# Block-sparse attention and a Fourier mixing layer on one core: whitened tiles fetched back one by one, turned tiles laid out tile by tile

## The chip, the core and the metric

The kernel runs on one core of one Trainium2 chip. A core has five engines with queues of their own: TensorE (PE in the profile, its weight loads PEld), VectorE (DVE), ScalarE (ACT), GpSimd (POOL), and SyncE (SP), which here issues nearly all DMA transfers. An engine takes its instructions in order; an instruction that waits for a semaphore holds up all that stand behind it on the same engine. The metric is the device time of one launch in microseconds.

## The reference

Four batches; in each, eight heads of attention over 768 positions, 64 wide, under a mask of 32 x 32 blocks. The output goes, as x of 768 x 512, through a Fourier mixing layer with a two-layer network behind it.

```python
scores = scale * np.matmul(q, k.transpose(0, 1, 3, 2))
scores = np.where(mask, scores, -1000000000.0)
attn = softmax(scores); attn_out = np.matmul(attn, v)
x = attn_out.transpose(0, 2, 1, 3).reshape(B, S, H * D)      # 4 x 768 x 512
u = x + np.real(np.fft.fft(np.fft.fft(x, axis=1), axis=2))
un = (u - mean(u)) / np.sqrt(var(u) + 1e-06)                 # along the 512
return u + np.maximum(un @ w_ch1, 0.0) @ w_ch2               # 512 x 2048, 2048 x 512
```

## The kernel before

**Tiles.** The 768 rows of a batch are two halves of three tiles of 128 rows (`half` 0 and 1, m = 0, 1, 2, T = 3). The mixing layer works in place on `xA` and `xB`, one for each half. `across` and `arrive` add the transform, `spread` takes mean and variance of a tile (POOL makes the reciprocal root), `whiten` makes the whitened tile `un` (128 x 512).

**Turning.** The product with `w_ch1` needs the whitened rows turned, as `unT[half]`: 128 partitions (a slice of the 512 features), 4 slices k, 384 rows. In the last batch PE turns each tile (`un_flip`). In batches 0, 1 and 2 PE is spared: `un_blocks` (L1009 to L1016) transposes 32 x 32 blocks on DVE and writes the tile to memory (`far`, one SP transfer of 256 KB); when all six tiles are written, `un_back` (L1018 to L1029) reads both halves back with 2 x 4 SP transfers of 192 KB in runs of 32 numbers (128 bytes), which puts the blocks in their places.

**Products.** `quad` computes four 128 x 384 blocks of the hidden layer by seven products in place of eight (Winograd's scheme). It needs sums of the four quarters of the turned matrix: `right(j)`, j = 1 to 4, four DVE subtractions (L1057), each half of the features and 384 rows wide, 128 x 768 elements in batches 0 to 2. The first two products of a quad (`xp`, `yp`) read `unT` as it is; the third (`z`) needs `right` 1 and 2, later ones 3 and 4. `channels` is the second layer, six tiles y in a round of two quads (L1268), four rounds in a batch. A round may instead be done by seven products on 256 columns (`round_of`, L1211, with sums on POOL, DVE and ACT): `seven[r]` is set if `state["alone"]` holds when the round's first quad is issued, and never for the last round.

**Order.** The order on every engine is written out by the program itself. Attention of batch b + 1 is interleaved with the mixing of batch b. A planner keeps a clock for each engine (`when`) with prices in the code. `late` holds the quads and channel steps that still are to be issued (PE's big work), `apart` the steps that prepare the next batch, each with a number `need`: it may go only when `len(late)` is not larger. The steps of list `before` in `mixer` (transform, whitening, `un_blocks`) carry a number that always allows them; those of `after` (`un_back`, the sums of weights `left`, `right`) carry `hold` = 6: they wait until only the last six channel steps of the batch in work are left, since `unT` has two buffers and the quads of the batch in work read both. `gap` takes steps from `apart` as long as the planner's DVE clock is not too far ahead of PE's. A step of kind "b" (`right`) is also held until PE's or DVE's clock is near `state["back"]`, which `un_back` sets to now + `BACK[b]` (13, 12, 15 us).

**Attention around it.** For each pair of heads and 128 keys a unit: `scores` (L579, two units are a group of 8 matmuls in the trace), ACT `Exp`, then, once channel steps are being issued, a DVE product with the mask (L609, tile `e`), in the first phase a mask product on PE (L589) instead; POOL adds up `e` (L639) and `values` (L653, tile `o`) multiplies with v. Scores have two PSUM slots, so a unit waits until `e` of the unit two before is made. A finished `o` is transposed by DVE into `oT` (L661, one buffer), and SP carries it to its place through memory (`row<-oT` L692, `x<-row` L696). SP also loads q, k and v (L231, L271) and stores the output (L1279).

**Also touched.** `scale_x` (L766) divides x by the sums of the softmax (kind "d", six steps a batch), `invert` (tile `st`, L751) turns the sums on PE before it, `spare_room` gives `right` and `left` their space. `general`, a second path for large scores, is not taken with these inputs.

Of the kernel before, what the change touches and what calls it, by code (L numbers as in the profile page):

```python
# [11 lines left out]
FP32 = mybir.dt.float32  # L12
# [87 lines left out]
def kernel(  # L100
# [14 lines left out]
    nc = tc.nc  # L115

    B, H, S, D = q.shape
    DM = H * D
    FF = w_ch1.shape[1]
    P = 128  # L120
    C = S // P
    BLK = 32
    NB = S // BLK
    NR = sampled_blocks.shape[1]
    HS = S // 2
    KS = cos_s.shape[1]
    KD = cos_d.shape[1]
    ND = DM // P
    NF = FF // P
    T = C // 2  # L130
# [51 lines left out]
    tr_p = ctx.enter_context(tc.tile_pool(name="tr_p", bufs=2))  # L182
# [3 lines left out]
    far_p = ctx.enter_context(tc.tile_pool(name="far_p", bufs=1, space=bass.MemoryType.DRAM))  # L186
# [7 lines left out]
    when = {"PE": 0.0, "ACT": 0.0, "DVE": 0.0, "POOL": 0.0}  # L194
# [18 lines left out]
    def room(i, shape, name, dtype=FP32):  # L213
        return big.tile(shape, dtype, tag=f"big{i}", name=name)
# [86 lines left out]
    def bit(n):  # L301
# [5 lines left out]
                      in_=bass.AP(tensor=_words(sampled_blocks, NB * NR), offset=0,  # L307
                                  ap=[[0, NB], [1, 2 * NB * NR]]))
# [135 lines left out]
    for w, w_sb in ((w_ch1, w1_sb), (w_ch2, w2_sb)):  # L444
        rows, cols = w.shape
        words = _words(w, rows * cols)
        for row in range(rows // P):
            for col in range(0, cols, WN):
                src = bass.AP(tensor=words, offset=2 * (row * P * cols + col),
                              ap=[[2 * cols, P], [1, 2 * WN]])  # L450
# [532 lines left out]
    def mixer(b, xA, xB):  # L983


        uns, unT = {}, {}
# [2 lines left out]

        def un_flip(half, m):  # L990
            if half not in unT:
                unT[half] = tr_p.tile([P, ND, T * P], FP32, tag="tr", name="unT")
            un = uns.pop((half, m))
            tag, pool = (("t", ps_t), ("m", ps_m))[half == 1 and m != 0]
            tp = pool.tile([P, ND, P], FP32, tag=tag, name="utp")
            for d in range(ND):
                nc.tensor.transpose(tp[:, d, :], un[:, d * P:(d + 1) * P], ident)
            nc.scalar.copy(out=unT[half][:, :, m * P:(m + 1) * P], in_=tp)

# [3 lines left out]

        lines = {}

        def un_blocks(half, m):  # L1010

            un = uns.pop((half, m))
            if half not in lines:
                lines[half] = far_p.tile([T, P, DM], FP32, tag=f"un{half}", name="far")
            nc.vector.transpose(out=un, in_=un)
            nc.sync.dma_start(out=lines[half][m], in_=un)  # L1016

        def un_back():  # L1018

            for half in range(2):  # L1020
                unT[half] = tr_p.tile([P, ND, T * P], FP32, tag="tr", name="unT")
                of = lines[half].rearrange("m (g j) (k a i) -> a j k (m g) i",
                                           j=BLK, a=P // BLK, i=BLK)
                for a in range(P // BLK):
                    nc.sync.dma_start(
                        out=unT[half][BLK * a:BLK * a + BLK].rearrange(
                            "j k (g i) -> j k g i", i=BLK),
                        in_=of[a])
            state["back"] = max(when["PE"], state["ready"]) + BACK[b]  # L1029

        t, s = {}, {}
        K1, K2 = slice(0, ND // 2), slice(ND // 2, ND)

        def spare_room():
            if s:
                return
            rest, n, w = room(5, [P, ND * HS], "t4"), HS * ND // 2, P * ND // 2
            t[4] = rest[:, 0:n].rearrange("p (k n) -> p k n", n=HS)
            for i in (1, 3, 4):
                s[i] = rest[:, n:n + w].rearrange("p (k n) -> p k n", n=P)  # L1040
                n += w

        def right(j, *tiles):

            spare_room()
            if 1 not in t:
                both = room(4, [P, ND, HS], "t12")
                t[1], t[2], t[3] = both[:, K1, :], both[:, K2, :], unT[1][:, K1, :]
            b11, b21 = unT[0][:, K1, :], unT[0][:, K2, :]
            b12, b22 = unT[1][:, K1, :], unT[1][:, K2, :]  # L1050

            def part(ap):
                return ap.rearrange("p k (t n) -> p k t n", n=P)[:, :, tiles[0]:tiles[-1] + 1, :]

            to, a, c = {1: (t[1], b12, b11), 2: (t[2], b22, t[1]), 3: (b12, b22, b12),
                        4: (t[4], b21, t[2])}[j]
            tt(out=part(to), in0=part(a), in1=part(c), op=ALU.subtract)  # L1057
# [24 lines left out]
        def quad(p):  # L1082

            g = p // 2 % 2 if last else 0
            if p % 2 == 0:
                for i in range(2):
                    hs[g, i] = room((2, 0)[g] + i, [P, 4, HS], "h" + "AB"[i])
            if not last:
                if p % 2 == 0:
                    seven[p // 2] = state["alone"] and p // 2 < NF // 4 - 1  # L1090
                elif seven[p // 2]:
                    state["drain"]()
                    sums_room()
                    for j in (1, 2, 4, 3):
                        round_right(p // 2, j)
            l1, l2 = 2 * (p % 2), 2 * (p % 2) + 1
            h11, h12, h21, h22 = (hs[g, i][:, l, :] for l in (l1, l2) for i in range(2))
            a11, a12, s2, a22 = blocks(p)
            b11, b21, b22 = unT[0][:, K1, :], unT[0][:, K2, :], unT[1][:, K2, :]

            def product(to, a, c, after=0.0):
                for k in range(ND // 2):
                    nc.tensor.matmul(to, a[:, k, :], c[:, k, :], start=(k == 0),  # L1103
                                     stop=(k == ND // 2 - 1))
                return busy("PE", PRODUCT, after) + HOP

            def plus(to, ps, a, at):
                tt(out=to, in0=ps, in1=a, op=ALU.add)  # L1108
                return busy("DVE", SUM, at) + HOP

            def relu(h, at):
                nc.scalar.activation(out=h, in_=h, func=ACT.Relu)  # L1112
                busy("ACT", RELU, at)

            def combine(j):
                left(p + 1, j)
                busy("DVE", COMBINE)

            x, at = ps_m.tile([P, 512], FP32, tag="m", name="xp")[:, 0:HS], bank("m")
            z5, z7 = (ps_s.tile([P, 2, 512], FP32, tag="s", name=name)[:, 0, 0:HS]  # L1120
                      for name in ("z5", "z7"))
            done = product(x, a11, b11)
            nc.scalar.copy(out=h11, in_=x)
            p1 = busy("ACT", RELU, done) + HOP
            give(at, p1 - HOP)
            y, at = ps_m.tile([P, 512], FP32, tag="m", name="yp")[:, 0:HS], bank("m")
            p2 = product(y, a12, b21)
            done = product(z7, s2, t[2])
            u2 = plus(h21, z7, h11, max(done, p1))
            c11 = plus(h11, y, h11, p2)  # L1130
            relu(h11, c11)
            done = product(z5, s[1], t[1])
            plus(h12, z5, h21, done)
            combine(1)
            done = product(z7, s[3], t[3], u2)
            u3 = plus(h21, z7, h21, done)
            c22 = plus(h22, z5, h21, done)
            z_at[0] = c22
            relu(h22, c22)
            combine(3)  # L1140
            gap(0.0, 1.9)
            done = product(y, a22, t[4], c11)
            c21 = plus(h21, y, h21, done)
            give(at, c21 - HOP)
            relu(h21, c21)
            gap(0.0, 1.9, "t")
            done = product(z7, s[4], b22, u3)
            z_at[1] = plus(h12, z7, h12, done)
            relu(h12, z_at[1])
            combine(4)  # L1150
            if last:
                for j in ((1, 2), (3, 4))[p % 2]:
                    output_right(p // 4, j, p // 2 % 2)
            elif p % 2 == 1 and seven[p // 2]:
                state["soon"] = 0.4
# [243 lines left out]
        le = [("d", lambda i=i: left(0, i), 0.0, 0.0, COMBINE) for i in (1, 3, 4)]  # L1399
# [3 lines left out]
        if not last:  # L1403
            before = first + [pq[1], ar[0][1], ar[1][1], sp[0][1],
                              pq[2], wh[0][1], ft[0][1], ar[0][2], ar[1][2], sp[0][2],
                              pq[0], wh[0][2], ft[0][2], ar[0][0], ar[1][0], sp[0][0],
                              sp[1][1], wh[0][0], ft[0][0], sp[1][2], wh[1][1], ft[1][1],
                              sp[1][0], wh[1][2], ft[1][2], wh[1][0], ft[1][0]]
            after = ([("-", un_back, 0.0, 0.0, 0.0)] + le +
                     [("b", lambda i=i: right(i, 0, 1, 2), 0.0, 0.0, 1.0 if b else 1.7)  # L1410
                      for i in (1, 2, 3, 4)])
        rest = []
        for r in range(2 if last else 0):
            rest += [(lambda p=p: quad(p), 7 * PRODUCT) for p in range(4 * r, 4 * r + 4)]
# [12 lines left out]
    MOST, LEAST = 9.6, 2.5  # L1427
    COVER = 100.0
    AHEAD = 2.2
    BACK = 13.0, 12.0, 15.0  # L1430
    ALONE = 3.0
    LEAVES = 13.0
    SP = UP // SLOT
# [396 lines left out]
```

## Time and profile before

| what | value |
|---|---|
| median of 3 runs | 1061.15 us (1060.93 to 1061.73) |
| the profiled execution, its own time | 1062.32 us |
| its span, first to last instruction | 1060.2 us |
| mean granted TensorE clock | 0.986 |
| DVE busy | 712.8 us, 67% |
| ACT, POOL busy | 373.2 us, 327.3 us |
| `y` L1268, 336 matmuls of 512 columns | 75.2 + 75.1 us in two groups |
| `z<-unT,t` L1103, 256 matmuls of 384 columns | 93.3 us |
| `far<-un` / `unT<-far` | 18 transfers of 256 KB / 24 of 192 KB |

The span is divided as the program is: first attention of batch 0 alone (the first `scale_x` starts at 135.8 us), then phases in which the mixing of one batch overlaps with attention of the next, and at the end the mixing of the last batch alone (the last `scale_x` starts at 803.6 us). A line of the view in order of time gives start, duration, engine, source line, operation, output and inputs, count, and in brackets how long the engine was idle before it and what released it.

### The profile page before, as it was taken

What the parts mean: (1) busy time and instruction counts of PE and PEld (TensorE: products, weight loads), DVE (VectorE), ACT (ScalarE), POOL (GpSimd) and SP (SyncE); (2) the same over time, 40 slices, a digit from 0 to 9 for tenths busy, and PEclk for the clock granted to TensorE, in tenths of its full rate; (3) what the DMA queues carried; (4) which work ended last, traced back from release to release, by engine and by line L of the source; (5) the groups of instructions that cost most, each with busy time, mean ns of one, the idle gap of its engine ahead of it and who ended that gap; (6) DMA issues with size and microseconds to landing.
All of it is one profiled execution on the core that took longest, in us unless ns stands there. A gap on an engine that the chain in (4) does not pass through costs nothing.

```text
span 1060.2 us, 13059 instructions
## 1 busy us (share of the span) xinstructions
PE 1014.9 (96%) x4526; PEld 564.1 (53%) x4526; DVE 712.8 (67%) x1292; ACT 373.2 (35%) x763; POOL 327.3 (31%) x363
## 2 busy tenths in 40 slices
PE   8999999999999999799999999869999999999996
PEld 4333345435776853344544764334454764578575
DVE  6898795969776567574579477656357575674663
ACT  6978755563122223343241223333120221210210
POOL 1000183565733306373354222743340221000000
PEclk9999999999999999899999999989999999999998
DMA  7857522292000014732120002731000001000001
GB/s 213 233 168 220 113 46 45 50 141 35 1 1 1 1 46 115 104 64 46 30 45 1 1 11 72 137 65 23 11 18 10 1 1 41 19 1 1 0 17 47
DMA packets 163461, 58.12 MB, mean 55 GB/s; under 512 B 144172, under 2 KB 154170, under 8 KB 163386
## 3 DMA queue, kind: packets, MB, share of 16 engines
q1 hardware_dynamic: 162134, 56.45, 23.9%
q8 instruction: 38, 0.62, 0.3%
q10 hardware_dynamic: 1220, 0.72, 0.3%
q14 instruction: 37, 0.30, 0.1%
q0 software_dynamic: 32, 0.01, 0.0%
HBM read 43.80 MB, written 13.37 MB: 54 GB/s over the span
## 4 chain that ended last, share of the span: by engine, by line
PE 82%; DVE 7%; ACT 3%; POOL 2%; DMA 2%; issue 2%; SPq 2%; DVEq 0%; ACTq 0%; POOLq 0%
PE z L1103 16%; PE y L1268 12%; PE s L579 10%; PE o L653 8%; PE yp L1103 8%; PE yy L1336 7%; PE xp L1103 4%; PE yz L1211 3%; PE yw L1211 2%; PE yc L1211 2%; PE zp L861 2%; DVE e L609 1%; POOL acc L639 1%; PE s L589 1%; ACT e L599 1%
## 5 line engine op out<-in xcount | busy, mean ns | idle before, releaser
L639 POOL TENSOR_TENSOR acc<-acc,e 128x384 f32<-128x384 f32 x162 | 165.8, 1056 | 84.8 <-DVE e L609 62.2
L579 PE MATMUL s<-qT,kT 64*128 64x384 f32 x768 | 157.6, 525 | 28.8 <-DVE e L609 22.3
L653 PE MATMUL o<-e,vr 128*64 128x384 f32 x768 | 143.0, 499 | 0.0
L579 PEld LDWEIGHTS s<-qT,kT 64*128 64x128 f32 x768 | 64.7, 188 | 112.2 <-DVE e L609 42.7
L607 ACT ACTIVATE s<-s 128x768 f32<-128x768 f32 x86 | 65.7, 793 | 133.2 <-PE s L579 125.7
L639 POOL TENSOR_TENSOR acc<-e 128x384 f32<-128x384 f32 x40 | 44.7, 1137 | 212.7 <-ACT e L599 125.2
L609 DVE TENSOR_TENSOR e<-s,mask 128x768 f32<-128x768 f32 x86 | 78.3, 948 | 36.7 <-ACT s L607 31.1
L599 ACT ACTIVATE e<-s 128x768 f32<-128x768 f32 x106 | 80.9, 811 | 53.3 <-PE s L589 34.9
L1103 PE MATMUL z<-unT,t 128*128 128x384 f32 x256 | 93.3, 487 | 0.8 <-DVE hA L1108 0.8
L653 PEld LDWEIGHTS o<-e,vr 128*64 128x64 f32 x768 | 48.0, 137 | 71.0 <-issue 68.6
L1108 DVE TENSOR_TENSOR hA<-z,hA 128x384 f32<-128x384 f32 x64 | 35.6, 556 | 67.0 <-PE z L1103 66.9
L1112 ACT ACTIVATE hA<-hA 128x384 f32<-128x384 f32 x64 | 33.5, 523 | 123.4 <-DVE hA L1108 123.4
L1268 PE MATMUL y<-w_sb,hB 128*128 128x512 f32 x168 | 75.2, 596 | 0.0
L1268 PE MATMUL y<-w_sb,hA 128*128 128x512 f32 x168 | 75.1, 595 | 0.0
L1224 POOL TENSOR_TENSOR x<-of,x 128x256 f32<-128x256 f32 x45 | 34.8, 780 | 125.2 <-ACT of L1216 85.2
L1103 PEld LDWEIGHTS z<-unT,t 128*128 128x128 f32 x256 | 48.4, 190 | 35.6 <-DVE hA L1108 2.4
L1271 DVE TENSOR_TENSOR x<-y,x 128x512 f32<-128x512 f32 x42 | 28.9, 688 | 54.8 <-PE y L1268 54.8
L1112 ACT ACTIVATE hB<-hB 128x384 f32<-128x384 f32 x64 | 33.5, 523 | 86.3 <-DVE hB L1108 86.3
L1268 PEld LDWEIGHTS y<-w_sb,hB 128*128 128x128 f32 x168 | 31.1, 190 | 38.8 <-issue 38.6
L1268 PEld LDWEIGHTS y<-w_sb,hA 128*128 128x128 f32 x168 | 31.1, 190 | 37.3 <-issue 36.0
L1103 PE MATMUL xp<-unT,w_sb 128*128 128x384 f32 x128 | 49.9, 515 | 0.0
L1103 PE MATMUL yp<-unT,w_sb 128*128 128x384 f32 x128 | 47.4, 493 | 0.0
(236 smaller groups left out, 1703.8 us busy)
## 6 DMA issues: line engine op xcount, KB each, us to landing
wraw<-in_moe_w_ch_dram SPq DMA_DIRECT2D x32, 512.0 KB
vr<-in_v_dram SPq DMA_DIRECT2D x30, 192.0 KB
far<-un SPq DMA_DIRECT2D x18, 256.0 KB
unT<-far SPq DMA_DIRECT2D x24, 192.0 KB
qb<-in_q_dram SPq DMA_DIRECT2D x44, 96.0 KB
kb<-in_k_dram SPq DMA_DIRECT2D x44, 96.0 KB
out_dram<-x SPq DMA_DIRECT2D x11, 252.0 KB
out_dram<-x SPq DMA_DIRECT2D x18, 128.0 KB
```

Of the source, the lines that this page charges most:

```text
L579: nc.tensor.matmul(s[:, i, 0:HS], kT[rows, c * P:(c + 1) * P], qT[rows, queries], start=True, stop=u not in by_pe)
L599: nc.scalar.activation(out=e, in_=s[:, :, 0:HS], func=ACT.Exp, scale=scale)
L607: nc.scalar.activation(out=s[:, :, 0:HS], in_=s[:, :, 0:HS], func=ACT.Exp, scale=scale)
L609: nc.vector.tensor_tensor(out=e, in0=s[:, :, 0:HS], in1=m.broadcast_to([P, 2, HS]), op=ALU.mult)
L639: nc.gpsimd.tensor_add(out=acc[:, i, :], in0=start[:, i, :], in1=e[:, i, :])
L653: nc.tensor.matmul(o[D * i:D * i + D, :], vt[:, i, c, :], e[:, i, :], start=(c == 0), stop=(c == C - 1))
L1103: nc.tensor.matmul(to, a[:, k, :], c[:, k, :], start=(k == 0), stop=(k == ND // 2 - 1))
L1108: tt(out=to, in0=ps, in1=a, op=ALU.add)
L1112: nc.scalar.activation(out=h, in_=h, func=ACT.Relu)
L1211: nc.tensor.matmul(to, a[:, k, :], c[:, k, :], start=start and k == 0, stop=k == 1, skip_group_check=True)
L1268: nc.tensor.matmul(y, hs[0, half][:, l, m * P:(m + 1) * P], w2_sb[:, 4 * r + l, :], start=(l == 0), stop=(l == 3))
L1336: nc.tensor.matmul(ps, a[:, k, :], c[k // 2][:, k % 2, :] if isinstance(c, list) else c[:, k, :], start=(k == 0), stop=(k == 3))
```

## The change

`far` becomes one tile of memory for each (half, m). `un_blocks` appends each written tile to a queue `sent`; as soon as fewer than six steps are left in `late`, a call first fetches every tile that was queued before it, so a tile is fetched one tile after it was written. `fetch` reads one tile with four transfers of 64 KB, again in runs of 128 bytes. `un_back` fetches what is left and sets `state["back"]` to now + 9 us. `unT` is laid out tile by tile (128 x 3 x 4 x 128); the 384 columns of a product are three runs of 128. `right` is called for tiles 1 and 2 first, all four sums, then `un_last` adds 2 us to `state["back"]`, then for tile 0. `un_flip` of the last batch and `quad` follow the new layout.

```diff
-            nc.scalar.copy(out=unT[half][:, :, m * P:(m + 1) * P], in_=tp)
+            nc.scalar.copy(out=unT[half][:, m, :, :], in_=tp)
...
-        lines = {}
+        lines, sent = {}, deque()
+
+        def fetch(half, m):
+            if half not in unT:
+                unT[half] = tr_p.tile([P, T, ND, P], FP32, tag="tr", name="unT")
+            of = lines[half, m].rearrange("(g j) (k a i) -> a j k g i",
+                                          j=BLK, a=P // BLK, i=BLK)
+            for a in range(P // BLK):
+                nc.sync.dma_start(
+                    out=unT[half][BLK * a:BLK * a + BLK, m, :, :].rearrange(
+                        "j k (g i) -> j k g i", i=BLK),
+                    in_=of[a])
 
         def un_blocks(half, m):
             un = uns.pop((half, m))
-            if half not in lines:
-                lines[half] = far_p.tile([T, P, DM], FP32, tag=f"un{half}", name="far")
+            lines[half, m] = far_p.tile([P, DM], FP32, tag=f"un{half}{m}", name="far")
             nc.vector.transpose(out=un, in_=un)
-            nc.sync.dma_start(out=lines[half][m], in_=un)
+            nc.sync.dma_start(out=lines[half, m], in_=un)
+            while sent and len(late) < 2 * T:
+                fetch(*sent.popleft())
+            sent.append((half, m))
 
         def un_back():
-            for half in range(2):
-                unT[half] = tr_p.tile([P, ND, T * P], FP32, tag="tr", name="unT")
-                of = lines[half].rearrange("m (g j) (k a i) -> a j k (m g) i",
-                                           j=BLK, a=P // BLK, i=BLK)
-                for a in range(P // BLK):
-                    nc.sync.dma_start(
-                        out=unT[half][BLK * a:BLK * a + BLK].rearrange(
-                            "j k (g i) -> j k g i", i=BLK),
-                        in_=of[a])
-            state["back"] = max(when["PE"], state["ready"]) + BACK[b]
+            while sent:
+                fetch(*sent.popleft())
+            state["back"] = max(when["PE"], state["ready"]) + BACK[0]
+
+        def un_last():
+            state["back"] += BACK[1]
...
+        def by_k(half, ks):
+            return unT[half][:, :, ks, :].rearrange("p m k n -> p k m n")
...
             def part(ap):
-                return ap.rearrange("p k (t n) -> p k t n", n=P)[:, :, tiles[0]:tiles[-1] + 1, :]
+                return ap[:, :, tiles[0]:tiles[-1] + 1, :]
...
-            after = ([("-", un_back, 0.0, 0.0, 0.0)] + le +
-                     [("b", lambda i=i: right(i, 0, 1, 2), 0.0, 0.0, 1.0 if b else 1.7)
-                      for i in (1, 2, 3, 4)])
+            on = [[("b", lambda i=i, m=m: right(i, *m), 0.0, 0.0, us) for i in (1, 2, 3, 4)]
+                  for m, us in (((1, 2), 1.2), ((0,), 0.7))]
+            after = ([("-", un_back, 0.0, 0.0, 0.0)] + le + on[0] +
+                     [("-", un_last, 0.0, 0.0, 0.0)] + on[1])
...
-    BACK = 13.0, 12.0, 15.0
+    BACK = 9.0, 2.0
```

More of the change, by code (lines that the diff above doesn't have):

```diff
@@ L997, in un_flip @@
                 nc.tensor.transpose(tp[:, d, :], un[:, d * P:(d + 1) * P], ident)
-            nc.scalar.copy(out=unT[half][:, :, m * P:(m + 1) * P], in_=tp)
-        lines = {}
+            nc.scalar.copy(out=unT[half][:, m, :, :], in_=tp)
+        lines, sent = {}, deque()
+        def fetch(half, m):
+            if half not in unT:
+                unT[half] = tr_p.tile([P, T, ND, P], FP32, tag="tr", name="unT")
+            of = lines[half, m].rearrange("(g j) (k a i) -> a j k g i",
[5 more added lines that the diff above has]
+                    in_=of[a])
@@ L1018, in un_back @@
+            sent.append((half, m))
         def un_back():
-            for half in range(2):
-                unT[half] = tr_p.tile([P, ND, T * P], FP32, tag="tr", name="unT")
-                of = lines[half].rearrange("m (g j) (k a i) -> a j k (m g) i",
-                                           j=BLK, a=P // BLK, i=BLK)
-                for a in range(P // BLK):
-                    nc.sync.dma_start(
-                        out=unT[half][BLK * a:BLK * a + BLK].rearrange(
-                            "j k (g i) -> j k g i", i=BLK),
-                        in_=of[a])
@@ L1037, in spare_room @@
             rest, n, w = room(5, [P, ND * HS], "t4"), HS * ND // 2, P * ND // 2
-            t[4] = rest[:, 0:n].rearrange("p (k n) -> p k n", n=HS)
+            t[4] = rest[:, 0:n].rearrange("p (k m n) -> p k m n", m=T, n=P)
             for i in (1, 3, 4):
@@ L1045, in right @@
             spare_room()
+            b11, b21, b12, b22 = (by_k(h, ks) for h in range(2) for ks in (K1, K2))
             if 1 not in t:
[L1047 to L1050, printed above, removed]
+                both = room(4, [P, ND, T, P], "t12")
+                t[1], t[2], t[3] = both[:, K1], both[:, K2], b12
             def part(ap):
-                return ap.rearrange("p k (t n) -> p k t n", n=P)[:, :, tiles[0]:tiles[-1] + 1, :]
+                return ap[:, :, tiles[0]:tiles[-1] + 1, :]
             to, a, c = {1: (t[1], b12, b11), 2: (t[2], b22, t[1]), 3: (b12, b22, b12),
@@ L1098, in quad @@
             a11, a12, s2, a22 = blocks(p)
-            b11, b21, b22 = unT[0][:, K1, :], unT[0][:, K2, :], unT[1][:, K2, :]
+            b11, b21, b22 = by_k(0, K1), by_k(0, K2), by_k(1, K2)
             def product(to, a, c, after=0.0):
                 for k in range(ND // 2):
-                    nc.tensor.matmul(to, a[:, k, :], c[:, k, :], start=(k == 0),
+                    nc.tensor.matmul(to, a[:, k, :], c[:, k], start=(k == 0),
                                      stop=(k == ND // 2 - 1))
```

## The prediction

> **What bounds the kernel now.** I read the page's engine rows and its chain first, then PE in order of time, looking for bracketed waits, then DVE and SP at the same moments, and last the DMA load.
>
> ```profile
> PE 1014.9 (96%) x4526; PEld 564.1 (53%) x4526; DVE 712.8 (67%) x1292; ACT 373.2 (35%) x763; POOL 327.3 (31%) x363
> ...
> PE 82%; DVE 7%; ACT 3%; POOL 2%; DMA 2%; issue 2%; SPq 2%; DVEq 0%; ACTq 0%; POOLq 0%
> ```
>
> PE is the bound. The time is PE's work plus PE's waits, so an edit counts only if it alters one of the two. After 150 us PE has two long waits, both where one batch's quads follow another's. Batch 1, PE and then DVE:
>
> ```profile
> 429.48 1.78 PE L579 MATMUL s<-qT,kT 64*128 64x384 f32 x8 [1.29 <-DVE e L609]
> 431.18 2.80 PE L653 MATMUL o<-e,vr 128*64 128x384 f32 x16
> 440.15 2.93 PE L579 MATMUL s<-qT,kT 64*128 64x384 f32 x8 [6.17 <-DVE e L609]
> 443.01 2.93 PE L1103 MATMUL xp<-unT,w_sb 128*128 128x384 f32 x4
> ```
>
> ```profile
> 428.49 1.79 DVE L609 TENSOR_TENSOR e<-s,mask 128x768 f32<-128x768 f32 x2
> 435.54 0.96 DVE L1057 TENSOR_TENSOR t<-unT 128x768 f32<-128x768 f32 x1 [5.26 <-DMA unT<-far]
> ...
> 439.14 1.81 DVE L609 TENSOR_TENSOR e<-s,mask 128x768 f32<-128x768 f32 x2
> ```
>
> PE waits for `e`, `e` stands on DVE behind `right`, and `right` waits for the fetched tiles. After the wait PE runs at half speed: 8 score matmuls take 2.93 us, `xp` 2.72 (443.01 to 445.73) where 1.29 is usual. Batch 2, PE, DVE and SP:
>
> ```profile
> 682.74 1.78 PE L579 MATMUL s<-qT,kT 64*128 64x384 f32 x8 [1.29 <-DVE e L609]
> ...
> 697.93 2.93 PE L579 MATMUL s<-qT,kT 64*128 64x384 f32 x8 [8.40 <-DVE e L609]
> ```
>
> ```profile
> 692.86 0.58 DVE L661 STREAM_TRANSPOSE oT<-o 128x384 f32<-128x384 f32 x1 [5.57 <-DMA row<-oT]
> 693.36 0.91 DVE L1057 TENSOR_TENSOR t<-unT 128x768 f32<-128x768 f32 x1
> ```
>
> ```profile
> 673.69 11.10 SPq L1025 DMA_DIRECT2D unT<-far  x8
> 684.89 3.54 SPq L231 DMA_DIRECT2D qb<-in_q_dram  x4
> 688.53 2.74 SPq L692 DMA_DIRECT2D row<-oT  x4
> ```
>
> ```profile
> 676.00:680.00 4.00, 4.00 (x24) 1.54 (x22) 3.18 (x5) 1.74 (x3) 3.62 (x5) 1.00 1.00 132
> ```
>
> Here DVE waits because `oT` has one buffer, whose copy stood on SP behind eight fetches (11.1 us). The last columns of the window are clock, DMA share 1.00 and 132 GB/s: the burst of fetches is limited by the DMA engines, 1.5 MB in 11.1 us, not by SP.
>
> **The change, batch 1.** From the last quad's end (382.42) to the next quad 60.6 us pass. Their work: six y of 3.44 (20.6), three `pq` (2.1), nine score groups of 1.49 (13.4), o (9.8), `xt` and `sp` (1.6), 47.5 in all. So 13.1 are lost there, and 1.6 in the slow `xp` and `yp`: 14.7. Built, the changed kernel has on PE between these quads y y y, s, xt, s, o, s, y, sp, y, y: 27.7 us of work and one wait like that of 0.90 at 404.18. With Q for the last quad's end, the next quad is due at Q+28.6. Are the tiles there? Five tiles are written while `late` still holds six steps or more, so nothing is fetched early: SP issues all 24 fetches together behind the sixth write. DVE ends that tile at Q+4.9 (statistics .65, whiten .55, wait for POOL, whiten .55, y sum .69, transpose .71), three stores hold SP until Q+5.7, the write until Q+6.1. Twenty of 24 fetches at the burst's pace take 9.4 us and land 3.7 later (in the trace: last issue over at 431.8, DVE released at 435.54): tiles 1 and 2 at Q+19.2, tile 0 at about Q+21.1. On DVE `right` stands behind the sum of the fourth y, at Q+21.7, so it does not wait, and the first `z`, at Q+31.2, finds its sums made: the last needs 5.4 us of DVE from the tiles' arrival, so there are 6.6 us to spare. Six score groups move between later quads, where the trace has four groups and their o's in 11.81 us for 11.57 of work; I charge 0.4. Gain 14.7 - 0.9 - 0.4 = **13.4**.
>
> **Batch 2.** Lost now: 1.29 + 8.40, the slow groups 1.44 (2.93 for 1.49) and 0.67 (16 o matmuls 3.40 for 2.73): 11.8. Changed, four tiles are fetched between the writes. Moving down SP's rows with 2.2 to 2.4 us for four fetches (0.55 each, as `qb` loads of 96 KB cost at the least; a `row` transfer of 48 KB costs 0.62), each group delays the stores and `kb` loads behind it; the last write goes out at 675.2 in place of 673.3, and the last eight fetches are out at 680. Tiles 1 and 2 land near 680, tile 0 near 683. On DVE `right` for tiles 1 and 2 stands before `e` of the eighth group: after `kT` (681.76) 4 x 0.68 (the 512-wide rows of the last batch), then 0.95 of `e`: the next group starts at 685.4, PE having been free since 681.2. A wait of 4.2 replaces 1.29 and 8.40. `row<-oT` goes out by 686 and lands by 688, before `oT` is wanted (690). The other two groups follow the first quad. Gain 7.6; PE's clock may drop in 4.2 us of idling: in the windows it fell about 2.5 us into the wait of 8.40 and 5.4 into that of 6.17, each drop costing some 2.5; I take 1.5 of it. Gain **6.1**.
>
> The Trainium skill (TensorE: Matmul & The Clock Gate, "Why this matters for your kernels") warns of gaps over about 3 us. By it the drop comes for certain and the gain is 5.1; by the waits of 1.69 and 1.29, after which groups ran at speed, only short gaps are safe.
>
> **Batch 0.** Nothing waits here now, and this is where the change costs. Tiles come some 7 us sooner, so the planner puts the first quad before the last score groups, and DVE gets, one behind another from 234.0: four 512-wide sums, two 256-wide, the softmax sums (L708), two more, one `acc`, the reciprocal, and five `scale_x`, before the quad's first addition. Next to POOL `right` took 1.56 to 1.76 here against 0.95 later, a factor 1.7: 4 x 0.68 x 1.7 + 2 x 0.42 x 1.7 + 0.5 = 6.5, so `st` waits until 240.6 and not 239.6: **1.0**. Then 1.4 + 0.9 + 0.4 + 5 x 0.8 (0.68 to 0.93 alone) brings the addition to an end at 247.9; the product that needs it is due at 246.1: **1.8**. With 1.71 a `scale_x` (the pair of 3.42 at 254.5) it would be 6.3; POOL has no weight sums here now, so I take the low end.
>
> **Rounds.** This first quad no longer runs with `alone` set, so one round goes from 84 matmuls of 256 columns (0.2165 each, 18.2 us) to 48 of 512 (0.4295, 20.6): **+2.4**. One mask group of PE goes to DVE: **-0.4**. Folds of the next batch must now fit behind two quads and this round; they need about 20 us of DVE beside 20.6 of PE: **+0.3**.
>
> **At nothing.** Two-part sums cost DVE 4.4 for 3.8 us a batch, under PE's quads (without that cover 0.6 a batch). 48 more transfers and SP's waits for each write to land (before the next fetch) hold `qb`, `kb`, `vr`, `row` and stores behind them; in batch 0 `qb` slips from 219 to 222 and is wanted by ACT at 228.45. The last batch's turned tiles keep their sizes. A product over three runs of 128 columns has no row; three separate matmuls of 128 (0.110 each) would be 0.330 for 0.322, at most 8 ns on 512 matmuls, 4.1 us; none shorter is conceivable. The two-run DVE rows scale with size alone, so I take 0.
>
> **Sum:** -13.4 - 6.1 + 2.8 + 2.4 - 0.4 + 0.3 = -14.4. Span 1060.2 becomes 1045.8; the profiled execution, 1062.32 with 2.1 around the span, 1047.9. It lay 1.2 above the runs' median, so the median becomes **1046.8**.
>
> **Rivals.**
> *The wait in batch 2 stays as a wait for tiles* (SP's chain slips: four `kb` loads took 6.81 us at 658.15, where two 256 KB writes had just gone out, and more traffic may do the same to fetches; against: DMA share there is 0.36). Gain of batch 2 gone: 1053.
> *Batch 0 takes the dear `scale_x`* (6.3 for 1.8) and a clock drop (2.5): 1054. For: DVE rows doubled beside POOL; against: POOL's list has fewer sums there.
> *A fetch costs per transfer, not per byte* (slower). Place: SP's 24 issues in batch 1. At the 1.29 us that a fetch takes now, twenty take 25.8, tiles 1 and 2 land at Q+35.6, 9.8 later than the Q+25.8 that `z` allows, and the clock drops: batch 1 gains 0.9, not 13.4; batch 2's tiles come 12 later and its gain of 6.1 becomes a loss of 4: -14.4 + 12.5 + 10.1 = +8.2, 1069. It begins to hurt at 0.86 us a fetch and undoes the gain near 1.15. For: equal times of six of the eight fetches. Against: the first two, before the engines fill, take 0.65 and 0.77, and 48 KB takes 0.62.
> The Trainium skill (DMA: Bandwidth & Descriptors, "Anatomy of one DMA", for transfers that GpSimd issues) gives each a fixed 2 us; were none of it overlapped, 24 would take 48. The 0.62 of back-to-back rows says that it overlaps.
> *It does not do what it says*: in batch 1 nothing is fetched one by one, and if the order there brings the same wait, batch 2's gain pays for batch 0 and the round: about 1060.
>
> **Chances.** Forecast 0.58 (1041 to 1051), batch 2's wait 0.15, batch 0 0.09, price per transfer 0.14, no effect 0.04. The range 1041 to 1058 holds the first three. 0.2% (2 us) is what a measurement can tell from no change. Faster 0.82, same 0.04, slower 0.14.
>
> **What would show it.** Right: batch 1's quads about 29 us behind the last quad of batch 0, no DVE wait for `unT` over 1 us, fetch rows near 0.5 us, four rounds of `yc`, PE waits of 1 to 2 us before `st` and the third `z` of batch 0, one of about 4 us in batch 2. Wrong: fetch rows over 0.9 us, half clock before a batch's first quad, `L1103` rows above 486 ns with `unT` moving.

## The result: slower by 1.1 per cent, and the profile after

| what | before | after |
|---|---|---|
| median of 4 runs | 1061.26 us (1060.93 to 1061.73) | 1072.91 us (1072.56 to 1073.99) |
| ratio to before, 95% interval | | 1.0111 (1.0094 to 1.0129) |
| span of the profiled execution | 1060.2 us | 1072.0 us |
| mean granted clock | 0.986 | 0.979 |
| rounds of seven products, of all | 5 | 4 |

The prediction was 1046.8 us and faster. The time is 11.7 us longer, not 14.4 shorter.

The engine rows and the chain of the changed kernel's page:

```profile
PE 1020.5 (95%) x4486; PEld 557.9 (52%) x4486; DVE 712.6 (66%) x1294; ACT 369.4 (34%) x754; POOL 305.7 (29%) x344
...
PE 79%; DVE 11%; SPq 3%; ACT 3%; issue 2%; DMA 1%; POOL 1%; ACTq 0%; DVEq 0%
```

VectorE's busy time has not moved (712.8 before), but its share of the chain grew from 7 to 11 per cent: PE waits for it more, though it does not work more. The view of PE in order of time, changed kernel, between the quads of batch 0 and those of batch 1 (the last quad ends at 389.51):

```profile
423.72 2.93 PE L579 MATMUL s<-qT,kT 64*128 64x384 f32 x8 [17.79 <-DVE e L609]
426.58 5.20 PE L1280 MATMUL y<-w_sb,hB 128*128 128x512 f32 x8
...
439.46 1.45 PE L1115 MATMUL xp<-unT,w_sb 128*128 128x384 f32 x4
```

One wait of 17.79 us, and half clock behind it: eight score products take 2.86 us (1.49 is usual), eight of `y` 5.13 (3.44 is usual). Follow the bracket to VectorE, ScalarE and SP, the same view of each of these queues:

```profile
422.71 1.82 DVE L609 TENSOR_TENSOR e<-s,mask 128x768 f32<-128x768 f32 x2 [19.19 <-ACT s L607]
...
432.42 0.68 DVE L1069 TENSOR_TENSOR t<-unT 128x512 f32<-128x512 f32 x1
```

```profile
420.66 0.48 ACT L677 COPY x<-xt 128x384 f32<-128x384 f32 x1 [18.29 <-DMA out_dram<-x]
...
421.87 1.50 ACT L607 ACTIVATE s<-s 128x768 f32<-128x768 f32 x2
```

```profile
396.01 19.96 SPq L1016 DMA_DIRECT2D unT<-far  x24
416.08 2.50 SPq L1291 DMA_DIRECT2D out_dram<-x  x4
```

Read backwards: PE waits for `e`, `e` for the exponentials, and these stand on ScalarE behind the copy `x<-xt`. That copy begins the x of batch 2 in the buffer in which batch 0's x still lies (`xp` has two buffers), so it waits until batch 0's first half is stored. Four of these stores stand on SP behind 24 fetches, which hold it for 19.96 us. The fetched tiles themselves are in time: `t<-unT` at 432.42 waits for nothing.

While the block is issued, the windows (PE, its weight loads, VectorE, ScalarE and GpSimd in us, each with its count; then clock, DMA share, GB/s) show this:

```profile
404.00:408.00 4.00, 1.93 (x12) 0.48 (x8) 0.00 (x0) 0.00 (x0) 2.60 (x3) 1.00 0.62 97
...
412.00:416.00 4.00, 0.00 (x0) 0.00 (x0) 0.00 (x0) 0.00 (x0) 0.00 (x0) 0.50 0.62 97
```

The DMA engines are 62% busy, where the burst of batch 2 in the kernel before had 1.00. The block goes at SP's pace: 0.635 us (median of 72 rows) for a transfer of 64 KB. In this block twenty of the 24 took 0.58 to 0.64 us, and the second to the fifth 1.40 to 1.66, for a reason that no run here shows.

Batch 2, PE and then VectorE of the changed kernel:

```profile
703.72 2.93 PE L579 MATMUL s<-qT,kT 64*128 64x384 f32 x8 [5.29 <-DVE e L609]
```

```profile
698.73 1.46 DVE L1069 TENSOR_TENSOR t<-unT 128x512 f32<-128x512 f32 x1
700.23 1.36 DVE L1069 TENSOR_TENSOR t<-unT,t 128x512 f32<-128x512 f32 x1
701.51 0.68 DVE L1069 TENSOR_TENSOR unT<-unT 128x512 f32<-128x512 f32 x1
702.12 0.68 DVE L1069 TENSOR_TENSOR t<-unT,t 128x512 f32<-128x512 f32 x1
702.72 1.81 DVE L609 TENSOR_TENSOR e<-s,mask 128x768 f32<-128x768 f32 x2
```

This is the forecast wait: the four sums for tiles 1 and 2 stand ahead of `e`. Here no fetch is late either.

**Where the 11.8 us of span are.** For each row of PE take the distance to the start of the next row, less its count times the usual distance for its kind (lower quartile over the kernels of this study). What is left is waiting and slow clock. In us, by stretch; the two columns on the right are experiments below:

| stretch | before | after | after_back13 | back_13_12_9 |
|---|---|---|---|---|
| up to the second quad of batch 0 | 13.5 | 17.7 | 13.8 | 14.5 |
| rest of batch 0's quads | 3.5 | 2.5 | 3.2 | 3.0 |
| last quad of batch 0 to second of batch 1 | 16.1 | 23.0 | 12.2 | 13.1 |
| rest of batch 1's quads | 2.6 | 4.3 | 2.7 | 2.3 |
| last quad of batch 1 to second of batch 2 | 16.9 | 15.7 | 16.7 | 15.0 |
| from there to the end | 5.7 | 4.3 | 7.0 | 6.0 |

The sums are 58.3 before and 67.5 after, 9.2 more. With 2.4 for the round that is no longer done by seven products this makes 11.6 of 11.8. The sums of the two experiments, 55.6 and 53.9, lie 2.7 and 4.4 below the one before, while their spans are 4.3 and 4.0 shorter: a column is good to about 1.5 us.

### The profile page after: what moved, and what is told of

Same layout as the page of the kernel before. It is cut to its first block, busy times and chain, and to the rows that moved or that the text cites. A ratio compares the mean times of both kernels' runs of the same rounds, so it can differ in the third digit from the quotient of the medians.

```text
span 1072.0 us, 12982 instructions
## 1 busy us (share of the span) xinstructions
PE 1020.5 (95%) x4486; PEld 557.9 (52%) x4486; DVE 712.6 (66%) x1294; ACT 369.4 (34%) x754; POOL 305.7 (29%) x344
## 4 chain that ended last, share of the span: by engine, by line
PE 79%; DVE 11%; SPq 3%; ACT 3%; issue 2%; DMA 1%; POOL 1%; ACTq 0%; DVEq 0%
PE z L1115 15%; PE y L1280 14%; PE s L579 10%; PE o L653 8%; PE yp L1115 7%; PE yy L1348 6%; PE xp L1115 4%; PE yz L1223 3%; PE yw L1223 2%; PE zp L861 2%; PE yc L1223 2%; SPq L1016 2%; DVE t L1069 1%; PE sp L724 1%; DVE e L609 1%
## 5 line engine op out<-in xcount | busy, mean ns | idle before, releaser
L639 POOL TENSOR_TENSOR acc<-e 128x384 f32<-128x384 f32 x42 | 47.4, 1150 | 213.5 <-ACT e L599 125.2
L1280 PE MATMUL y<-w_sb,hB 128*128 128x512 f32 x192 | 87.1, 604 | 0.0
L1280 PE MATMUL y<-w_sb,hA 128*128 128x512 f32 x192 | 85.3, 595 | 0.0
L1283 DVE TENSOR_TENSOR x<-y,x 128x512 f32<-128x512 f32 x48 | 33.1, 690 | 61.2 <-PE y L1280 61.2
L1280 PEld LDWEIGHTS y<-w_sb,hB 128*128 128x128 f32 x192 | 36.3, 193 | 46.6 <-issue 46.1
L1280 PEld LDWEIGHTS y<-w_sb,hA 128*128 128x128 f32 x192 | 35.8, 190 | 44.1 <-issue 41.7
L1236 POOL TENSOR_TENSOR x<-of,x 128x256 f32<-128x256 f32 x36 | 26.4, 739 | 95.5 <-ACT of L1228 65.5
L1135 ACT COPY hA<-xp 128x384 f32<-128x384 f32 x32 | 15.3, 478 | 96.0 <-PE xp L1115 96.0
```

Of the source, the lines that this page charges most:

```text
L639: nc.gpsimd.tensor_add(out=acc[:, i, :], in0=start[:, i, :], in1=e[:, i, :])
L1280: nc.tensor.matmul(y, hs[0, half][:, l, m * P:(m + 1) * P], w2_sb[:, 4 * r + l, :], start=(l == 0), stop=(l == 3))
```

## The experiments

All are compared with the kernel before, run on the same chip. Theory A: the stores behind the fetches. Theory B: late tiles. Theories C and E: the order that the planner writes out. D: the new form of fetching.

**Stores on another queue** (act_stores).

```diff
-                store(half, m)
+                store(half, m, queue=nc.scalar)
```

> The changed kernel, but the output stores of batches 0 to 2 are issued on ScalarE's queue instead of SP's; every other instruction keeps its engine and its order. Theory A (the loss is the queue: four stores of batch 0's hA rows stand on SP behind 24 fetches, and ACT's copy x<-xt waits for them): the PE wait of 17.79 us at 423.72 shrinks to 2 to 3 us, the half clock behind it (some 3 us) goes, tile 0 may come 1 to 2 us late; batch 2's wait of 3.48 us of the same copy goes too. 1054 us, 1051 to 1058. Theory B (the 24 fetches themselves are late, the stores only happen to be the releaser): the same idle time comes back as a DVE wait for unT in front of the sums, 1068 us or more. Theory C (the lost seven-product round and the order of batch 0 are the loss): nothing changes, 1071 to 1074.

1066.53 us, 1.0048 (1.0031 to 1.0064). Better by 6.4 than the changed kernel, not by 19, and in none of the three ranges. The long wait became two of 4.5 us. SP in order of time, then ScalarE and VectorE, from an execution that took 1071.08 us:

```profile
397.46 34.44 SPq L1016 DMA_DIRECT2D unT<-far  x24
```

```profile
407.18 1.50 ACT L607 ACTIVATE s<-s 128x768 f32<-128x768 f32 x2 [13.78 <-DMA unT<-far]
```

```profile
429.83 0.69 DVE L1069 TENSOR_TENSOR t<-unT 128x512 f32<-128x512 f32 x1 [9.10 <-DMA unT<-far]
```

The 24 fetches now take 34.44 us, and now the tiles are late, as theory B has it. The reason stands in the program, and the semaphores in the trace's records of the transfers agree: all transfers, of whichever queue, mark their landing in eight counters in turn, so each waits for the one before it on its counter, and the two queues wait for each other's transfers. SP's fetches waited 12.4 us for stores here, and the exponentials of the row above stand behind stores on ScalarE that waited for a fetch. The move did not take the stores out of the fetches' way. The Trainium skill (DMA: Bandwidth & Descriptors, "Issuing engines are not separate DMA queues") says that issuing from several engines saves only the time to start a transfer; here the waits for each other's transfers left 6.4 of the 19 us that theory A expected.

**A shorter block in the same place** (burst8): batch 1 fetches as before, everything else as changed.

```diff
-            while sent and len(late) < 2 * T:
+            while sent and len(late) < 2 * T and b != 1:
...
+            if b == 1:
+                for half in range(2):
+                    fetch_half(half)
```

> The changed kernel, but batch 1 alone fetches as the kernel before did, eight transfers of 192 KB into the old layout, in the same place of every queue. It changes only how long SP is held ahead of the stores: 11.3 us in place of 20.0. Theory A: the wait of 17.79 us becomes about 9, the rest stays: 1064 us, 1062 to 1067. Theory C (order and round): 1071 to 1074. If a product over three separate runs of 128 columns cost PE anything, batch 1's z products would be shorter than the 487 ns of the changed kernel; expected equal.

1067.76 us, 1.0065 (1.0048 to 1.0082). SP, then PE:

```profile
396.20 14.21 SPq L1041 DMA_DIRECT2D unT<-far  x8
410.52 3.28 SPq L1312 DMA_DIRECT2D out_dram<-x  x4
```

```profile
418.94 2.93 PE L579 MATMUL s<-qT,kT 64*128 64x384 f32 x8 [12.84 <-DVE e L609]
```

The block took 14.2 us, not the 11.3 expected, and the median is just above its range. The block is 5.75 shorter than in the changed kernel, the wait 4.95 and the median 5.15. The wait follows the length of the block, and in both kernels the sums of the tiles wait for no fetch: that is theory A measured as a dose, at two lengths. Batch 1's `z` products, over one run of 384 columns here, take the same 1.45 us for four.

**One copy moved** (place_later): the queue of SP stays, only `x<-xt` goes behind one more pair of exponentials.

```diff
-                state["place"] = lambda: place(n, 0)
+                state["place"] = [2, lambda: place(n, 0)]
```

> The changed kernel with one step moved: ACT's copy x<-xt into the buffer whose stores are awaited (batches 2 and 3, half 0) comes one pair of score units later on ACT, behind their exponentials; fetches and stores stay as they are. Theory A: the wait of 17.79 us at 423.72 goes from the score products; xt holds the one PSUM bank that sp needs, so PE waits there instead, from some 410 to 421 us, about 10.8 us: 1063 us, 1060 to 1067. Theory B (tiles late): first quad of batch 1 not before 439, 1072 us.

1066.19 us, 1.0043 (1.0026 to 1.0060): 6.7 less than the changed kernel by moving one instruction on ScalarE (in batches 2 and 3) together with the three small transposes that feed it. ScalarE, then PE:

```profile
421.52 0.48 ACT L677 COPY x<-xt 128x384 f32<-128x384 f32 x1 [15.37 <-DMA out_dram<-x]
```

```profile
422.05 1.51 PE L738 MATMUL sp<-acc,pick 128*32 128x384 f32 x8 [9.71 <-ACT x L677]
```

The score products no longer wait. `sp` waits, since `xt` holds its PSUM bank, for 9.71 us where 10.8 were expected. Who stands behind the waiting copy pays; with that theory A is shown from the other end.

**The waiting times.** `BACK` 9 in the kernel before (before_back9), 13, 12, 15 in the changed kernel (after_back13), and each half alone.

```diff
-    BACK = 13.0, 12.0, 15.0
+    BACK = 9.0, 9.0, 9.0
```

> The kernel before with nothing changed but the three waiting times of the planner, 13, 12, 15 us, all set to 9, as in the changed kernel. By its written-out order it loses the seven-product form of batch 0's first round and puts the eight fetches of batch 1 ahead of the four stores. Theory A with order: batch 0 loses 3.2 and 2.4 us as in the changed kernel, batch 1 shows a wait of PE for e of about 9 us behind x<-xt where the changed kernel has 17.8: 1066 us, 1061 to 1071. Rival D (the new form of fetching is the whole cause, the waiting time is harmless): 1060 to 1062.

> The changed kernel with the waiting times of the kernel before (13, 12, 15 us, and 2 more for tile 0) in place of 9 and 2. Its written-out order keeps the seven-product form in batch 0's first round and puts the fetches of batch 1 one by one between the stores. Theory A with order: batch 0 as before the change, batch 1 without the long wait behind x<-xt, as batch 2 of the changed kernel: 1058 us, 1054 to 1062. Rival D (price per transfer: 48 more transfers at 0.68 us hold SP): 1066 us or more.

> The changed kernel with the waiting time of batch 0 alone put back from 9 to 13 us; batches 1 and 2 keep 9, tile 0 its 2. One number. Theory E (the loss is made in batch 0: with 9 us its first quad stands before the last score groups, its first round is not in seven products, the preparation of batch 1 runs ahead on the free VectorE, and so the 24 fetches stand in one block before the stores): five rounds of seven products again, fetches of batch 1 between the stores, no wait over 6 us there: 1056 us, 1051 to 1060. Rival (9 us is too short in batches 1 and 2 as well): 1064 or more.

> The reverse: batch 0 keeps 9 us, batches 1 and 2 get the old 13 (and 2 for tile 0). Theory E: the block of 24 fetches and the wait of PE of some 17 us behind x<-xt stay, four rounds of seven products: 1071 us, 1067 to 1075. Rival (9 us too short in batches 1 and 2): 1060 or less.

| kernel | fetched | waiting times | median, us | ratio, 95% |
|---|---|---|---|---|
| before | blocks | 13, 12, 15 | 1061.4 | |
| before_back9 | blocks | 9, 9, 9 | 1079.12 | 1.0162 (1.0145 to 1.0179) |
| after | one by one | 9, 9, 9 (and 2 for tile 0, as below) | 1072.91 | 1.0111 (1.0094 to 1.0129) |
| b_9_13_13 | one by one | 9, 13, 13 | 1069.87 | 1.0082 (1.0066 to 1.0099) |
| b_13_9_9 | one by one | 13, 9, 9 | 1059.11 | 0.9981 (0.9971 to 0.9991) |
| after_back13 | one by one | 13, 12, 15 | 1058.09 | 0.9970 (0.9960 to 0.9980) |

The edit has two halves of opposite sign. Fetching one by one gains 6.2 us with the short times and 3.3 with the old ones; the short times cost 17.7 without it and 14.8 with it. And of the three numbers batch 0's alone does it: 13.8 us between after and b_13_9_9. In the program written out with 9 there, the first quad stands before the last score groups and its round is not made by seven products; with 10 to 13 neither is so. Through which steps of the planner this puts batch 1's fetches into one block stays open (see round7). The expectations for after_back13, b_9_13_13 and b_13_9_9 held: the wait behind `x<-xt` is there in b_9_13_13, with 17.72 us, and b_13_9_9 has none over 5.29 in batch 1. That for before_back9 was 13 too low. Its wait in batch 1 is 13.01 us and not 9, and blocks arrive too late for a wait of 9 in batches 0 and 2 as well: there VectorE's first sum waits 5.02 and 7.61 us, until 4.4 to 4.5 us after the last fetch has left SP. Its PE, in order of time:

```profile
247.19 0.90 PE L751 MATMUL st<-ident,sums 128*128 128x128 f32 x3 [8.07 <-DVE sums L708]
...
426.58 2.93 PE L579 MATMUL s<-qT,kT 64*128 64x384 f32 x8 [13.01 <-DVE e L609]
...
710.49 2.93 PE L579 MATMUL s<-qT,kT 64*128 64x384 f32 x8 [12.67 <-DVE e L609]
```

**The round alone** (round7): the form of batch 0's first round forced back.

```diff
-                    seven[p // 2] = state["alone"] and p // 2 < NF // 4 - 1
+                    seven[p // 2] = (state["alone"] or b == p == 0 and len(late) > 0) and p // 2 < NF // 4 - 1
```

> The changed kernel with all its waiting times, but batch 0's first round is made in seven products all the same (48 products of 512 columns become 84 of 256). The written-out order then has only two tiles of batch 1 written before the first stores, and the fetches in groups between the stores. Theory E: what the lost form costs is not its 2.4 us on PE but the order behind it: both go, the wait of 2.0 before st in batch 0 stays: 1059 us, 1055 to 1064. Rival (the form costs its 2.4 us alone): 1070 us.

1076.68 us, 1.0143 (1.0126 to 1.0160): a miss by 17.7 us. The form changes where all later steps stand. As expected, batch 1's fetches now go out in groups of 8, 4, 4 and 8, but stores of each half still stand behind a group of 8. ScalarE:

```profile
409.81 0.48 ACT L677 COPY x<-xt 128x384 f32<-128x384 f32 x1 [6.56 <-DMA out_dram<-x]
...
444.79 0.48 ACT L677 COPY x<-xt 128x384 f32<-128x384 f32 x1 [10.63 <-DMA out_dram<-x]
```

Now both halves' copies wait for stores behind fetches, 6.56 and 10.63 us. So the form does decide whether the 24 stand in one block, but breaking up the block is not enough, and the link of theory E by which the loss goes with the form falls; the way in which stores are caught is the same.

**The price of small transfers where no store is caught** (block_13): after_back13, but nothing is fetched before all six tiles are written.

```diff
-            while sent and len(late) < 2 * T:
+            while sent and b < 0:
```

> As after_back13 (changed kernel, old waiting times), but no tile is fetched before all six are written: 24 transfers of 64 KB in one block behind the last write in batches 1 and 2, the stores of the first half ahead of them. It prices the small transfers where no store is caught. From the changed kernel's rows the block takes 20 us where the kernel before takes 11.3; the sums then come some 9 us later than in the kernel before, less the 3 us by which tiles 1 and 2 go first: 1061 + 2 x 5 = 1071 us, 1066 to 1076. Rival (what counts in this order is the bytes, not the number of transfers): 1059 to 1063.

1072.12 us, 1.0100 (1.0083 to 1.0117). SP, then VectorE and PE:

```profile
422.05 16.87 SPq L1016 DMA_DIRECT2D unT<-far  x24
```

```profile
438.40 0.69 DVE L1069 TENSOR_TENSOR t<-unT 128x512 f32<-128x512 f32 x1 [6.62 <-DMA unT<-far]
```

```profile
441.95 2.93 PE L579 MATMUL s<-qT,kT 64*128 64x384 f32 x8 [6.46 <-DVE e L609]
449.60 2.93 PE L579 MATMUL s<-qT,kT 64*128 64x384 f32 x8 [3.74 <-DVE e L609]
```

Small transfers in a block are dear: 0.70 us each (16.87 / 24), 5.6 us more for a block than the eight large ones before. What gains is fetching early; 14.0 us lie between block_13 and after_back13.

**The copy again, in the good order** (place_later13).

> after_back13 with the copy x<-xt of half 0 one pair of score units later, as in place_later. In after_back13 this copy waits 2.3 and 2.1 us only, so Theory A expects nothing of it: 1058 us, 1056 to 1060. If it gains more than 2 us, the copy's place costs something besides the stores.

1058.54 us, 0.9969 (0.9957 to 0.9982): nothing, as expected. The place of the copy costs only where stores are caught.

**Longer and mixed times** (back14: 13, 14, 14; back_13_12_9: 13, 12, 9).

> The changed kernel with 13 us in batch 0 and 14 in batches 1 and 2 (2 for tile 0). The written-out order then makes seven rounds in seven products (five before): 2 x 2.4 us less on PE. Fetches stand between the stores in batch 1; in batch 2 the stores of the first half come ahead of them. 1054 us, 1050 to 1060. Rival (a later preparation puts the fetches of batch 2 in one block and the sums late): 1062 or more.

1073.88 us, 1.0120 (1.0103 to 1.0137), a miss by 20. Seven rounds are made by seven products, but batch 2's tiles are prepared so late that PE itself waits for them:

```profile
742.16 2.90 PE L1115 MATMUL xp<-unT,w_sb 128*128 128x384 f32 x4 [9.27 <-DMA unT<-far]
...
752.57 2.90 PE L1115 MATMUL z<-t,w_sb 128*128 128x384 f32 x4 [5.44 <-DVE t L1069]
```

> The changed kernel with 13, 12 and 9 us for batches 0, 1 and 2 (2 for tile 0): the stretch between batches as after_back13 has it for batch 1 (12.2 us of waiting and slow clock from the last quad of batch 0 to the second of batch 1) and as b_13_9_9 has it for batch 2 (15.0 against 16.7). SP's order is the same in all three. If the stretches are independent of each other: 1058.1 - 1.7 - 0.9 = 1055.5 us, 1053 to 1058. Rival (the two stretches' differences are scatter between executions): 1058 to 1059.

1056.91 us, 0.9946 (0.9932 to 0.9960), inside its range: the fastest of the study, 16.0 below the changed kernel by three numbers. From after_back13 it is 1.2 us, and the two ratios' intervals meet at 0.9960, so the gain by the last number alone is barely told from scatter.

## Why the prediction was wrong, point by point

**The step that failed** is in batch 1: "27.7 us of work and one wait like that of 0.90 at 404.18". That wait came, with 0.76 us, and behind it one of 17.79 that the sum does not have. The prediction had that right which made it fail: all 24 fetches go out together behind the sixth write. It asked whether the *fetched tiles* would be late and did not ask what stands *behind* the block on SP and who waits for that: four stores, and behind them a buffer, a copy on ScalarE, the exponentials, `e`, PE. Where it puts the 48 added transfers at nothing it does name stores among what they hold up, but follows only `qb` of batch 0. In place of 13.4 gained the stretch lost 6.9 (23.0 against 16.1). These 20.3 us are most of the 26 by which the forecast missed.

**The pace of the fetches** was mis-sized: 0.47 us each, the rate of the DMA engines in the old burst, where SP needs 0.83 in this block (19.96 / 24) and 0.70 in block_13. That moved the end of the last fetch from about Q+17.4 to Q+26.5. What it would have cost alone cannot be read here, since the longer wait covers it. An estimate by the prediction's own sum: the first twenty fetches took 17.24 us in place of 9.4, which brings tiles 1 and 2 at about Q+27.0, 1.2 later than the Q+25.8 that `z` allows. (That sum begins to hurt at 0.80 us a fetch, 16.0 us for twenty, and not at the 0.86 that is written there.) The mistake was to read the limit from transfers three times as large.

**Batch 2**: the wait of 4.2 is 5.29, since the first two sums took 1.46 and 1.36 us beside POOL where 0.68 was reckoned (the factor that the prediction used in batch 0 was left out here), and half clock followed it, as feared. Before it stands a new wait of 0.60, behind a copy `x<-xt` that here too waited for stores, 3.48 us. A wait of 1.71 before that is old (1.69 in the kernel before), but this time half clock followed it. Gained 1.2 in this stretch and 1.4 behind it, not 6.1.

**Batch 0**: forecast 2.8 lost, measured 4.2 up to the second quad less 1.0 behind it, 3.2. `st` waits 2.00 and not 1.0, followed by slow rows; the wait of 1.8 before the third `z` is not in this profile. In that of burst8, where the clock stayed up, it is there with 1.73.

**The round**: 2.4 by 48 products more of 512 columns and 84 fewer of 256: four rounds of seven products, as written. Right in size, but counted as the only price of the order in which it was lost.

**At nothing**: the layout by tiles (`z<-unT,t` 487 ns in both kernels), VectorE's two-part sums (712.6 us against 712.8) and the longer SP queue in batch 0 held. -0.4 for the mask group and +0.3 for the folds are below what can be read apart.

**The rivals**: "a fetch costs per transfer" named the place and came within 4 us of the time (1069), by a way that was not taken: the tiles were not late, the stores were. Where no store is caught, in block_13, it is what happens. That nothing is fetched one by one in batch 1 ("it does not do what it says") was true as well.

## What to carry to other kernels

When transfers are added to a queue, list what stands behind them in that queue until the next idle moment, and follow each of these to the engine that waits for it, through buffers that must be stored before they are used again; the arrival of the added transfers is only half of the question. Take the price of a transfer from transfers of its own size, and look at the DMA share to see whether the queue or the DMA engines set it. Test a tuning constant and the edit that it was tuned with apart: here the edit alone gained 0.3 per cent, the constant lost more than four times as much, and set batch by batch the two together gained 0.5.

## What the hardware showed that was not expected

SP takes 0.635 us for most fetches of 64 KB in runs of 128 bytes (0.557 to 1.659), so three of them hold the queue longer than one of 192 KB, of which eight took 10.00 to 14.31 us.

Half clock came after waits of different lengths. In the changed kernel it followed the 2.00 us before `st`:

```profile
242.00:244.00 2.00, 2.00 (x6) 1.39 (x6) 2.00 (x3) 0.00 (x0) 2.00 (x3) 0.50 0.02 3
```

In burst8 the same wait of 2.00 left the clock alone. In batch 2 of the changed kernel it followed the 1.71 us that ended at 687.83; the 1.69 at the same place of the kernel before left it alone.

```profile
690.00:692.00 2.00, 2.00 (x9) 1.00 (x9) 2.00 (x3) 0.80 (x1) 2.00 (x2) 0.50 0.33 71
```

The Trainium skill (TensorE: Matmul & The Clock Gate, "Why this matters for your kernels") warns of idle gaps over about 3 us; these runs show one of 1.71 as enough at times.
